# One shared PSUM pool, joined bucket bits, and DMA transposes of the attention output in a fused attention and channel-mix kernel

## The chip, the cores and the metric

The kernel runs on one core of a Trainium2 chip. The metric is device time in microseconds (us). An execution usually takes 1.7 to 2.2 us more than the span of the profile, which runs from the first to the last instruction. Runs also carry the mean clock that the throttle granted to TensorE, as a share of full speed. Some executions of a kernel take longer at a lower clock (e11: 271.86 us at 0.981, the three others 265.93 to 266.20 us at 0.991 to 0.994). Those more than 1.5% above the fastest one of the same kernel count as slow. A median that is quoted with a run is that of all its executions; ratios, and comparisons unless it is said otherwise, use the fast ones alone.

Names: PE is TensorE (matmul), PEld its weight loads, DVE is VectorE, ACT ScalarE, POOL GpSimd, SP SyncE, the engine that issues nearly all DMAs here. PSUM is the memory that the matmuls write to; this kernel divides it into eight banks, each of 512 float32 values per partition.

## The reference

Sixteen *pairs* (4 batches x 4 pairs of heads; 768 positions, head size 64) of hash-bucketed attention feed a channel mix per batch. Cut to what matters:

```python
q_bits = (np.einsum('bhsd,dk->bhsk', q, proj) > 0)      # 6 bits; the same for k
mask = q_bucket[:, :, :, None] == k_bucket[:, :, None, :]
scores = np.where(mask, scale * q @ k.T, -1e9)
attn = softmax(scores) @ v                               # per head
x = attn.transpose(0, 2, 1, 3).reshape(B, S, 512)
x_prev = x shifted by one position, zeros first
xk = mu_k * x + (1 - mu_k) * x_prev                      # xr likewise, with mu_r
k = relu(xk @ w_k); v = (k * k) @ w_v; r = sigmoid(xr @ w_r)
out = r * v
```

The first four pairs (batch 0) are computed uncentred. From pair 4 on the values are centred: the mean of v is taken off before the attention and given back later.

## The kernel before

A small planner in the kernel takes operations with durations, priorities, dependences and PSUM slots, simulates the five engines, and fixes one order per engine. Its priorities (the table `PR`) were tuned against that simulation. The operations are then issued in the planned order to a recording layer (the tile framework), which notes what each instruction reads and writes and puts in the semaphore waits.

PSUM is two tiles of two banks for scores and four tiles of one bank for everything else:

```python
sc_t = [psum.tile([P, STEP], FP32, name=f"sc{i}", tag=f"sc{i}") for i in range(2)]   # STEP = 1024
sm_t = [psum.tile([P, 512], FP32, name=f"sm{i}", tag=f"sm{i}") for i in range(4)]
plan = Plan({"sc": (2, 2), "sm": (4, 3)})

def sm(name):
    return sm_t[plan.slot[name]]
```

Bucket bits are made in two halves of 384 columns, each in one small bank. An attention output (`ob`) is turned by six PE transposes; DVE evicts it to `xt` and adds the mean in the same operation. POOL copies one column block for the shift, and DVE mixes:

```python
def ft(nm=nm):                                  # PE, six transposes
    ps = sm(nm)[:, 0:HALF].bitcast(BF16)
    for c in range(NSC):
        nc.tensor.transpose(ps[:, c * P : (c + 1) * P], ob_t[so][:, c, :], idb)
def fx(nm=nm):                                  # DVE, evicts and adds the mean
    # ... (pairs 0 to 3: a plain copy)
    nc.vector.tensor_scalar(out=xt_t[sx][:, P:], in0=sm(nm)[:, 0:HALF].bitcast(BF16),
                            scalar1=mc_t[smc][:, 0:1], scalar2=None, op0=ALU.add)
# ...
def f1(mu=mu, dst=dst):                         # DVE, mix: mu * (x - x_prev) + x; mu holds mu - 1 here
    nc.vector.scalar_tensor_tensor(out=dst[smx], in0=df_t[sd], scalar=mu[:, t : t + 1], in1=x, op0=ALU.mult, op1=ALU.add)
```

The softmax here doesn't subtract the row's maximum and nothing guards it: scores larger than these inputs give would overflow.

## Time and profile before

| | before |
|---|---|
| time, median of 3 runs | 258.73 us (258.31 to 258.94) |
| span of the profile | 256.8 us, granted clock 0.993 |
| PE busy | 239.3 us, 93% |
| first mix matmul starts | 63.4 us |

The first lines are the page's part 1 (busy time of each engine, share of the span, instructions) and part 4 (the chain of waits that ended last, as shares of the span).

```profile
PE 239.3 (93%) x2519; PEld 143.5 (56%) x2519; DVE 195.1 (76%) x391; ACT 185.5 (72%) x242; POOL 57.9 (23%) x98
...
PE 63%; DMA 15%; DVE 10%; POOL 3%; SPq 3%; issue 2%; ACT 2%; POOLq 0%; DVEq 0%
```

Next, busy time of each engine by stretches: from:to in us and its length, then us busy (instructions) of PE, PEld, DVE, ACT and POOL, the granted clock, the DMA engines' busy share and GB/s.

```profile
20.00:60.00 40.00, 34.90 (x488) 22.35 (x487) 29.58 (x54) 34.54 (x37) 10.79 (x20) 0.98 0.94 177
60.00:100.00 40.00, 38.97 (x417) 23.91 (x416) 35.89 (x75) 32.03 (x45) 13.78 (x17) 1.00 0.95 187
100.00:180.00 80.00, 78.90 (x891) 48.20 (x888) 72.84 (x142) 63.75 (x80) 20.74 (x27) 1.00 0.83 206
180.00:220.00 40.00, 40.00 (x461) 25.98 (x460) 24.77 (x59) 32.62 (x45) 1.00 (x3) 1.00 0.09 34
```

From 60 us on PE is the limit: 38.97 of 40, 78.90 of 80, 40.00 of 40 us. From 20 to 60 us only attention is ready, and ACT's exponentials (144 of 1.03 us) and PE share the work. Groups of instructions (busy us, mean ns of one | idle us of the engine just before them, and what ended it) and then waits (total us, times, longest):

```profile
L652 PE MATMUL sm<-xk,wk 128*128 128x384 bf16 x256 | 48.9, 326 | 0.2
L681 PE MATMUL sm<-wv,k 128*128 128x512 bf16 x192 | 47.8, 379 | 1.1 <-DVE ob L599 1.1
...
L583 PE MATMUL sm<-va,pt 128*128 128x65 bf16 x1152 | 44.6, 193 | 0.0
...
L674 ACT ACTIVATE rs<-sm 128x512 f32<-128x512 f32 x24 | 14.4, 599 | 22.1 <-PE sm L671 18.9
```

```profile
ACT pt L557 <- PE sc L553: 28.3, 48, 3.9
...
PE sc L553 <- ACT pt L557: 4.5, 11, 0.7
...
PE sm L681 <- DVE ob L599: 1.1, 1, 1.1
```

PE's mix matmuls (L652 and L681) idle 0.2 and 1.1 us in the whole run. PE's largest wait for another engine is for a score buffer: 4.5 us.

### The profile page before, as it was taken

Reading aid. Unit: us, or ns where it says so; the run is one execution under the profiler, and the core shown is the slowest. Engines: PE = TensorE matmul, PEld = TensorE weight load, DVE = VectorE, ACT = ScalarE, POOL = GpSimd, SP = SyncE. Lnnn points to the kernel's source line nnn. Section 1 sums busy time; section 2 is a strip of 40 time slices with the busy share of each in tenths; the row PEclk is TensorE's granted clock in tenths of the full one; section 3 lists DMA queues with packets and bytes.
Section 4 is the critical chain, followed back from the end, with each engine's and each line's share of the span. In section 5 each row is a group of like instructions: output and inputs, shape, how many; then the busy total and the mean of one; then the engine's idle time right before and its main releaser. Section 6 shows DMA issues by size and latency. Waiting matters only on the chain.

```text
span 256.8 us, 6319 instructions
## 1 busy us (share of the span) xinstructions
PE 239.3 (93%) x2519; PEld 143.5 (56%) x2519; DVE 195.1 (76%) x391; ACT 185.5 (72%) x242; POOL 57.9 (23%) x98
## 2 busy tenths in 40 slices
PE   6768898888999999999999989999999999999994
PEld 2334564555666456656666655555666666555441
DVE  4999676777789997989998999898685753675322
ACT  3838888888994598878898967586798986147320
POOL 2491415056051330504041424040000000000000
PEclk9998999999999999999999999999999999999999
DMA  6968979799998479796978987888200011220132
GB/s 191 382 168 155 163 174 172 199 171 180 225 201 227 116 199 175 212 241 190 274 148 266 216 241 149 233 164 166 89 3 6 3 41 43 82 86 1 41 123 82
DMA packets 64565, 39.78 MB, mean 155 GB/s; under 512 B 46756, under 2 KB 60952, under 8 KB 64536
## 3 DMA queue, kind: packets, MB, share of 16 engines
q1 hardware_dynamic: 62248, 36.76, 58.4%
q0 software_dynamic: 2208, 2.62, 6.3%
q8 instruction: 19, 0.31, 0.5%
q14 instruction: 10, 0.08, 0.1%
q10 hardware_dynamic: 80, 0.00, 0.0%
HBM read 24.12 MB, written 6.29 MB: 118 GB/s over the span
## 4 chain that ended last, share of the span: by engine, by line
PE 63%; DMA 15%; DVE 10%; POOL 3%; SPq 3%; issue 2%; ACT 2%; POOLq 0%; DVEq 0%
PE sc L553 16%; PE sm L681 15%; PE sm L652 11%; PE sm L583 10%; DMA vn<-in_v_dram 8%; PE sm L671 7%; PE sm L443 4%; DMA qn<-in_q_dram 3%; DMA ak<-kh 2%; POOL vt L360 2%; DMA kn<-in_k_dram 2%; PE sm L609 2%; ACT pt L557 2%; SPq L334 1%; DVE xk L635 1%
## 5 line engine op out<-in xcount | busy, mean ns | idle before, releaser
L557 ACT ACTIVATE pt<-sc 128x1024 bf16<-128x1024 f32 x144 | 143.2, 1028 | 29.9 <-PE sc L553 28.3
L553 PE MATMUL sc<-aq,ak 128*128 128x512 f16 (+1 forms) x384 | 84.6, 329 | 4.5 <-ACT pt L557 4.5
L553 PEld LDWEIGHTS <-ak 128*128 128x128 f16 x384 | 33.6, 98 | 31.1 <-issue 12.2
L652 PE MATMUL sm<-xk,wk 128*128 128x384 bf16 x256 | 48.9, 326 | 0.2
L681 PE MATMUL sm<-wv,k 128*128 128x512 bf16 x192 | 47.8, 379 | 1.1 <-DVE ob L599 1.1
L583 PEld LDWEIGHTS <-pt 128*128 128x128 bf16 x1152 | 42.9, 97 | 9.0 <-issue 0.6
L583 PE MATMUL sm<-va,pt 128*128 128x65 bf16 x1152 | 44.6, 193 | 0.0
L656 ACT ACTIVATE kr<-sm 128x384 bf16<-128x384 f32 x64 | 31.3, 498 | 9.5 <-PE sm L652 7.5
L652 PEld LDWEIGHTS <-wk 128*128 128x128 bf16 x256 | 24.1, 98 | 15.2 <-issue 0.3
L360 POOL TENSOR_TENSOR vt<-vn 128x384 f32<-128x384 f32 x12 | 15.1, 1256 | 71.5 <-DMA vn<-in_v_dram 71.5
L659 DVE TENSOR_TENSOR k<-kr 128x384 bf16<-128x384 bf16 x64 | 23.8, 385 | 8.5 <-ACT kr L656 8.4
L674 ACT ACTIVATE rs<-sm 128x512 f32<-128x512 f32 x24 | 14.4, 599 | 22.1 <-PE sm L671 18.9
L681 PEld LDWEIGHTS <-k 128*128 128x128 bf16 x192 | 18.4, 98 | 19.5 <-issue 1.3
L688 DVE SCALAR_TENSOR_TENSOR os<-rs,sm 128x512 f32<-128x512 f32 x24 | 16.3, 684 | 16.5 <-PE sm L681 16.4
L671 PE MATMUL sm<-wr,xr 128*128 128x512 bf16 x96 | 24.6, 379 | 0.0
L619 POOL COPY xt<-xt 128x127 bf16<-128x127 bf16 x16 | 8.4, 525 | 69.1 <-DVE xt L615 64.4
L447 DVE TENSOR_SCALAR bx<-sm 128x384 uint16<-128x384 uint16 (+1 forms) x32 | 16.4, 549 | 3.3 <-PE sm L443 2.6
L599 DVE TENSOR_TENSOR ob<-sm,rc 128x384 bf16<-128x384 f32 x32 | 17.8, 556 | 0.9
L405 DVE SCALAR_TENSOR_TENSOR kh<-kn,kh 128x768 f16<-128x768 f32 x15 | 18.3, 1219 | 0.1
L635 DVE SCALAR_TENSOR_TENSOR xk<-df,muk,xt 128x768 bf16<-128x768 bf16 x16 | 16.7, 1046 | 0.3
L443 PE MATMUL sm<-ak,p 128*32 128x384 f16 x124 | 14.4, 335 | 2.3 <-DVE ak L422 1.3
L635 DVE SCALAR_TENSOR_TENSOR xr<-df,mur,xt 128x768 bf16<-128x768 bf16 x16 | 16.1, 1018 | 0.0
(76 smaller groups left out, 195.3 us busy)
## 6 DMA issues: line engine op xcount, KB each, us to landing
vn<-in_v_dram SPq DMA_DIRECT2D x16, 384.0 KB
out_dram<-os SPq DMA_DIRECT2D x24, 256.0 KB
qn<-in_q_dram SPq DMA_DIRECT2D x15, 384.0 KB
kn<-in_k_dram SPq DMA_DIRECT2D x15, 384.0 KB
wk<-in_moe_w_k_dram POOLq DMA_DIRECT2D x4, 256.0 KB, 5.3
wv<-in_moe_w_v_dram POOLq DMA_DIRECT2D x4, 256.0 KB, 8.7
wr<-in_moe_w_r_dram POOLq DMA_DIRECT2D x2, 256.0 KB, 5.4
aq<-bx SPq DMA_DIRECT2D x31, 9.0 KB
```

Of the source, the lines that this page charges most:

```text
L360: nc.gpsimd.tensor_tensor(out=vt[:, :, :, 0:E], in0=src[:, :, 0:3, 0:E], in1=src[:, :, 3:6, 0:E], op=ALU.add)
L405: nc.vector.scalar_tensor_tensor(out=nh[:, :, D:P], in0=nat.rearrange("p j (c d) -> p (j c) d", d=D), scalar=QS, in1=nh[:, :, 0:D], op0=AL ...
L443: nc.tensor.matmul(ps[32 * i : 32 * i + 32, 0:HALF], w_, a[:, i // 2, h * HALF : (h + 1) * HALF], start=st, stop=not st)
L553: nc.tensor.matmul(ps[:, lo - s * STEP : hi - s * STEP], side_a["k"][sa][:, j, jc * P : (jc + 1) * P], side_a["q"][sa][:, j, q0 : q0 + hi ...
L557: nc.scalar.activation(out=pt_t[sp][:, s * STEP : (s + 1) * STEP], in_=sc_t[plan.slot[nm]], func=AF.Exp, bias=EBIAS, scale=ESC)
L583: nc.tensor.matmul(oo[:, ic * 65 : ic * 65 + 65], pt_t[sp][:, o : o + P], va_t[sa][:, j, jc, 0 : D + 1], start=(not uc and ic == 0 and jc ...
L635: nc.vector.scalar_tensor_tensor(out=dst[smx], in0=df_t[sd], scalar=mu[:, t : t + 1], in1=x, op0=ALU.mult, op1=ALU.add)
L652: nc.tensor.matmul(ps[:, 0:HALF], wk_sb[:, d, fc * P : (fc + 1) * P], xk_t[mx[d]][:, h * HALF : (h + 1) * HALF], start=(d == 0), stop=(d = ...
L656: nc.scalar.activation(out=kr_t[sk], in_=sm(nm)[:, 0:HALF], func=AF.Relu, scale=0.5 ** 0.5)
L659: nc.vector.tensor_tensor(out=k2_t[s2][:, h * HALF : (h + 1) * HALF], in0=kr_t[sk], in1=kr_t[sk], op=ALU.mult)
L671: nc.tensor.matmul(sm(nr), xr_t[mx[d]][:, c * P : (c + 1) * P], wr_sb[:, d, :], start=(d == 0), stop=(d == NDC - 1))
L681: nc.tensor.matmul(sm(nv), k2_t[(b * NFC + fc) % NK2][:, c * P : (c + 1) * P], wv_sb[:, fc, :], start=(fc == 0), stop=(fc == NFC - 1))
```

## The change

Its intent: (1) one PSUM pool of four two-bank tiles. Scores take whole tiles, up to three at a time, and small outputs take halves of tiles. (2) The bucket bits of a pair are made in one two-bank tile and read by one DVE operation. (3) The outputs of pairs 4 to 14 are turned by DMA transposes, not by PE. (4) x stays centred, since the DVE eviction that added the mean falls away; the mean is added in the mix, by a `tensor_scalar` with two scalars and a `tensor_tensor`, and POOL writes minus the mean in front of the first position. (5) All priorities are tuned again. The diff, cut to its core (planner bookkeeping and names left out):

```diff
-    sc_t = [psum.tile([P, STEP], FP32, ...) for i in range(2)]
-    sm_t = [psum.tile([P, 512], FP32, ...) for i in range(4)]
-    plan = Plan({"sc": (2, 2), "sm": (4, 3)})
+    ps_t = [psum.tile([P, STEP], FP32, name=f"ps{i}", tag=f"ps{i}") for i in range(4)]
+    plan = Plan((0, 1, 2), (7, 6, 5, 4), {"sc": 3, "sm": 4}, 3)
     def sm(name):
-        return sm_t[plan.slot[name]]
+        b_ = plan.slot[name]
+        return ps_t[b_ // 2][:, (b_ % 2) * 512 : (b_ % 2) * 512 + 512]
...
-        for h in range(2):
-            nm = f"bits{n}_{h}"          # 384 columns each, in a small bank
+        nm = f"bits{n}"                  # 768 columns, in a two-bank tile
...
+    OT_PE = (0, 1, 2, 3, 15)
+        def fd_():
+            nc.sync.dma_start_transpose(out=xt_t[sx][:, P:].rearrange("p (c q) -> p c q", q=P),
+                                        in_=ob_t[so].rearrange("p c d -> p (c d)"))
+        if n in OT_PE:
             # six PE transposes and a DVE copy, as before
+        else:
+            add("SP", 1.2, n + PR["otd"], fd_, r=[("ob", so, 0), ("ob", so, 1)], w=[("xt", sx)], ...)
...
-                nc.vector.scalar_tensor_tensor(out=dst[smx], in0=df_t[sd], scalar=mu[:, t : t + 1], in1=x, ...)
+                nc.vector.tensor_scalar(out=tm_t[tm], in0=df_t[sd], scalar1=mu[:, t : t + 1], scalar2=mc[:, 0:1], op0=ALU.mult, op1=ALU.add)
+                nc.vector.tensor_tensor(out=dst[smx], in0=tm_t[tm], in1=x, op=ALU.add)
```

## The prediction

> **What bounds the kernel now.** TensorE, from about 60 us on: the windows show PE busy 19.2 to 20.0 of every 20 us (18.9 once). Busy times of pipelined matmuls overlap, so I check with start-to-start times from the timeline (384 columns 0.162 us, 512 columns 0.216, a 65-column attention matmul 0.0316, a 1024-column score step 0.43, 16 bucket-bit matmuls 0.77, six transposes 0.335). With the counts per window these sum to about 152 us of the last 157: PE is 97% full. Over the whole span (256.8 us) they sum to about 225. The other 32 us are the start (some 12), the attention-only stretch of 20 to 60 us (some 9: no mix matmul is ready, ACT does exponentials of 1.03 us, busy 34.5 of 40), small gaps and the tail. In that stretch ACT loses 5.5 us, nearly all waiting for scores (waits): there are two score buffers, and 36 attention matmuls take 1.14 us, longer than one exponential.
>
> **What the change does.**
> - PE: 11 of 16 output transposes leave (pairs 4 to 14): 11 x 0.335 = 3.7 us, in the full stretch, so nearly all counts.
> - DVE: 11 evictions of 0.61 us leave (6.7). Bucket bits: two of 0.55 become one of about 0.95 (-2.4 in all). [...] In sum -12 of 195 us, mostly off the critical path: PE hardly waits for DVE.
> - DMA: 11 transposes of 192 KB. Those of before (384 KB) move about 210 GB/s with the queue full (174 to 176 us), where stores reach 400 (184 us): about 0.9 us each, 10 us between 75 and 185 us, where the share is about 0.85; it rises to about 0.95. [...] SP gains about 1 us of issue per pair.
> - PSUM: scores may hold three buffers, though the joined bits borrow one about 2 us per pair. From 20 to 60 us this should return 1 to 2.5 us of ACT's idle time, and start the first mix earlier by that.
>
> **Sum.** 3.7 us of PE work and 1.5 us of early idle time, less 0.3 us for late DMAs: 258.7 - 4.9 = 253.8 us. Range 250.0 to 257.5. Faster by over 2% (below 253.6) 0.46, within 2% 0.48, slower 0.06.
>
> **What would show it.** 30 output transposes on PE instead of 96; PE still full after 60 us; ACT's wait for scores from 20 to 60 us below 5.5; first mix matmul before 63 us; [...] DVE busy near 183; DMA share near 0.95 from 80 to 180 us; new waits of POOL's copy or df for a DMA, but few of PE.
>
> **What would make it wrong.** Queued transposes delaying the query and key transposes behind them, so that PE, in its fixed order, stalls on scores; SP waiting in order for an attention output and holding back loads; joined bits taking a score buffer when it is needed; shared banks adding waits between mix and scores; or the retuned priorities being worth more than I give them, seen as less idle time before 60 us.

The forecast's DVE sum came to -12 us, and its "DVE busy near 183" is 195 less that; only 9.1 us of it stand above (6.7 for evictions, 2.4 for bits), since the mix's term is cut. The 253.8 us is whole: no term of 3.7, 1.5 and 0.3 us is cut. The 0.95 us for the joined bits was an estimate; before's trace gives about as much (384 columns 549 ns, one column of another `tensor_scalar` out of PSUM, the mean's, 146: twice the difference and 146 make 952).

## The result, and the profile after

| | before | after |
|---|---|---|
| time, median | 258.60 us (258.31 to 258.94, 4 runs) | 289.77 us (289.29 to 291.15, 4 runs, all fast) |
| span, granted clock | 256.8 us, 0.993 | 287.5 us, 0.982 |
| PE busy | 239.3 us, 93% | 246.0 us, 86% |
| first mix matmul | 63.4 us | 72.2 us |

The ratio is 1.12 (95% interval 1.116 to 1.124). Ratios here and below are the mean time of one kernel's fast runs over that of the other's fast runs in the same rounds, so they are not quite the ratio of the medians quoted.

The same views of the kernel after, in the same order:

```profile
PE 246.0 (86%) x2453; PEld 142.9 (50%) x2453; DVE 189.8 (66%) x388; ACT 183.9 (64%) x242; POOL 60.8 (21%) x110
...
PE 53%; DVE 23%; DMA 10%; ACT 5%; issue 5%; POOL 1%; SPq 1%; ACTq 0%; DVEq 0%; POOLq 0%
```

```profile
20.00:60.00 40.00, 31.72 (x426) 20.74 (x426) 27.52 (x45) 28.54 (x31) 12.65 (x21) 0.91 0.88 180
60.00:100.00 40.00, 35.00 (x369) 21.20 (x368) 28.00 (x59) 31.93 (x44) 14.85 (x22) 0.96 0.79 166
100.00:180.00 80.00, 70.38 (x768) 41.80 (x767) 60.95 (x129) 55.92 (x71) 16.32 (x27) 1.00 0.73 176
180.00:220.00 40.00, 36.77 (x375) 21.68 (x374) 30.07 (x68) 27.77 (x38) 5.53 (x10) 1.00 0.59 138
```

```profile
L690 PE MATMUL ps<-xk,wk 128*128 128x384 bf16 x256 | 49.1, 329 | 4.9 <-ACT kr L694 2.2
L719 PE MATMUL ps<-wv,k 128*128 128x512 bf16 x192 | 47.6, 378 | 5.2 <-ACT rs L712 2.4
...
L601 PE MATMUL ps<-va,pt 128*128 128x65 bf16 x1152 | 48.4, 195 | 8.7 <-DVE va L404 2.3
...
L712 ACT ACTIVATE rs<-ps 128x512 f32<-128x512 f32 x24 | 14.4, 600 | 35.5 <-DVE os L726 15.1
```

```profile
ACT rs L712 <- DVE os L726: 15.1, 5, 3.3
...
PE ps L596 <- DVE ob L617: 5.2, 3, 2.2
...
PE ps L719 <- ACT rs L712: 2.4, 5, 0.7
...
PE ps L601 <- DVE va L404: 2.3, 4, 0.7
...
PE ps L719 <- DVE ob L617: 2.0, 4, 1.1
```

The loss is spread over the whole kernel: from 60 to 220 us PE was busy 142.15 us, not 157.87 (sums of the three stretches). PE's share of the chain fell from 63% to 53%, and DVE's rose from 10% to 23%. DMA did not take it: its busy share from 100 to 180 us fell from 0.83 to 0.73.

The waits name the reason. L719 is the last matmul of the channel mix, `k2 @ w_v`. It reads `k2` and `wv`; it does not read `rs` (ACT's gate, L712) or `ob` (an attention output, L617). Yet it waits for both. L712 is an evicting activation with two output buffers, and it waits 15.1 us for L726, DVE's product of another PSUM output. These are not waits for a free buffer: in the built program, each of the 7 has L712 writing one buffer while L726 reads the other. None of the five kinds of wait shown is in the list of before, except L681's single 1.1 us on `ob`. The timeline of one stretch shows it at work (start, us, instruction, and in brackets the engine's idle time before it and what ended it):

```profile
115.28 0.17 DVE L612 TENSOR_SCALAR rc<-ps 128x6 f32<-128x6 f32 x1 [1.33 <-PE ps L719]
115.48 0.19 DVE L613 RECIPROCAL rc<-rc 128x6 f32<-128x6 f32 x1
115.71 0.56 DVE L617 TENSOR_TENSOR ob<-ps,rc 128x384 bf16<-128x384 f32 x1
...
116.32 1.02 PE L719 MATMUL ps<-wv,k 128*128 128x512 bf16 x4 [1.07 <-DVE ob L617]
```

DVE normalises an attention output (L612, L613, L617; 115.28 to 116.27 us) out of one half of a two-bank tile. PE's next matmuls go into a different bank, the other half, and start 0.05 us after DVE is done. They had waited 1.07 us. DVE itself had idled 1.33 us before L612, released by PE's matmuls L719, whose result it doesn't read.

### The profile page after: what moved, and what is told of

Same layout as the page of the kernel before. It is cut to its first block, busy times and chain, and to the rows that moved or that the text cites. A ratio compares the mean times of both kernels' runs of the same rounds, so it can differ in the third digit from the quotient of the medians.

```text
span 287.5 us, 6215 instructions
## 1 busy us (share of the span) xinstructions
PE 246.0 (86%) x2453; PEld 142.9 (50%) x2453; DVE 189.8 (66%) x388; ACT 183.9 (64%) x242; POOL 60.8 (21%) x110
## 2 busy tenths in 40 slices
DMA packets 73366, 41.94 MB, mean 146 GB/s; under 512 B 55557, under 2 KB 69753, under 8 KB 73337
## 4 chain that ended last, share of the span: by engine, by line
PE 53%; DVE 23%; DMA 10%; ACT 5%; issue 5%; POOL 1%; SPq 1%; ACTq 0%; DVEq 0%; POOLq 0%
PE ps L719 12%; PE ps L571 10%; PE ps L690 10%; PE ps L601 9%; PE ps L709 6%; DMA qn<-in_q_dram 5%; PE ps L462 4%; DVE kh L424 3%; DVE ob L617 3%; ACT kr L694 3%; DVE va L404 3%; DMA vn<-in_v_dram 3%; DVE os L726 2%; DVE qh L424 2%; DVE qh L421 2%
## 5 line engine op out<-in xcount | busy, mean ns | idle before, releaser
L575 ACT ACTIVATE pt<-ps 128x1024 bf16<-128x1024 f32 x144 | 140.2, 1029 | 33.6 <-PE ps L571 32.9
L571 PE MATMUL ps<-aq,ak 128*128 128x512 f16 (+1 forms) x384 | 80.0, 330 | 2.3 <-DVE bx L465 1.5
L601 PEld LDWEIGHTS <-pt 128*128 128x128 bf16 x1152 | 45.8, 99 | 27.7 <-issue 19.6
L601 PE MATMUL ps<-va,pt 128*128 128x65 bf16 x1152 | 48.4, 195 | 8.7 <-DVE va L404 2.3
L690 PE MATMUL ps<-xk,wk 128*128 128x384 bf16 x256 | 49.1, 329 | 4.9 <-ACT kr L694 2.2
L719 PE MATMUL ps<-wv,k 128*128 128x512 bf16 x192 | 47.6, 378 | 5.2 <-ACT rs L712 2.4
L694 ACT ACTIVATE kr<-ps 128x384 bf16<-128x384 f32 x64 | 29.3, 492 | 24.0 <-PE ps L690 14.7
L712 ACT ACTIVATE rs<-ps 128x512 f32<-128x512 f32 x24 | 14.4, 600 | 35.5 <-DVE os L726 15.1
L719 PEld LDWEIGHTS <-k 128*128 128x128 bf16 x192 | 18.2, 97 | 26.3 <-issue 8.0
L726 DVE SCALAR_TENSOR_TENSOR os<-rs,ps 128x512 f32<-128x512 f32 x24 | 16.4, 682 | 21.6 <-PE ps L709 12.6
L709 PE MATMUL ps<-wr,xr 128*128 128x512 bf16 x96 | 24.6, 378 | 0.8 <-DVE ob L617 0.6
L617 DVE TENSOR_TENSOR ob<-ps,rc 128x384 bf16<-128x384 f32 x32 | 17.8, 556 | 4.8 <-PE ps L690 1.7
L465 DVE TENSOR_SCALAR bx<-ps 128x768 uint16<-128x768 uint16 (+1 forms) x16 | 15.3, 955 | 6.6 <-PE ps L462 6.3
L404 DVE SCALAR_TENSOR_TENSOR va<-ps,vn 128x384 bf16<-128x384 f32 x24 | 12.9, 553 | 8.9 <-ACT pt L575 2.2
L462 PE MATMUL ps<-aq,p 128*32 128x512 f16 (+1 forms) x124 | 15.1, 353 | 0.7 <-DVE bx L465 0.3
```

The costliest lines, as they stand in the source:

```text
L462: nc.tensor.matmul(ps[32 * i : 32 * i + 32, lo:hi], w_, a[:, i // 2, lo:hi], start=st, stop=not st)
L571: nc.tensor.matmul(ps[:, lo - s * STEP : hi - s * STEP], side_a["k"][sa][:, j, jc * P : (jc + 1) * P], side_a["q"][sa][:, j, q0 : q0 + hi ...
L575: nc.scalar.activation(out=pt_t[sp][:, s * STEP : (s + 1) * STEP], in_=ps_t[plan.slot[nm]], func=AF.Exp, bias=EBIAS, scale=ESC)
L601: nc.tensor.matmul(oo[:, ic * 65 : ic * 65 + 65], pt_t[sp][:, o : o + P], va_t[sa][:, j, jc, 0 : D + 1], start=(not uc and ic == 0 and jc ...
L617: nc.vector.tensor_tensor(out=ob_t[so][:, :, j * D : (j + 1) * D], in0=oo[:, :, 0:D], in1=rc_t[sr][:, 1, :].unsqueeze(2).to_broadcast([P, ...
L690: nc.tensor.matmul(ps[:, 0:HALF], wk_sb[:, d, fc * P : (fc + 1) * P], xk_t[mx[d]][:, h * HALF : (h + 1) * HALF], start=(d == 0), stop=(d = ...
```

## The experiments

**Theory 1: shared tiles.** Two halves of one tile are different banks to the planner, but the recording layer makes accesses of one half wait for accesses of the other. The planner knows banks singly, so its order neither expects nor avoids these waits. **Rivals.** Theory 2: the DMA transposes come late or hold up loads. Theory 3: the retuned order or the joined bits starve PE by themselves.

A count comes first, since it costs no run. In the built programs I resolved each semaphore wait to the instruction that it waits for, and noted where their only common memory is the *other* half of a PSUM tile:

```
kernel                                         waits resolved   other half only
before                                         1142             0
before with its small banks as halves (e2)     1096             205
after                                          1089             140
after, waits between halves declared away (e1) 1150             8
```

The 8 left belong to whole-tile operations. When this text was checked, the kernels were built again and counted with a slightly wider rule, which also takes two reads of one tile: 0, 235, 162 and 11. By it all 7 waits of L712 on L726 are of this kind, though both only read the tile, and so are all 6 of L601 on L404, 4 of 8 of L719 on L712, 2 of 4 of L719 on L617, 2 of 4 of L596 on L617 and 1 of 3 of L612 on L719. The others wait for the same half, as they must. So most, not all, of the waits shown above are of this kind. Whether they cost 31 us only a run can tell.

### e1: after, without the waits between halves

The same instructions in the same order on every engine; the layer is told that an access of one half need not wait for accesses of the other half, but for those that the plan itself orders (cut to its core, comments added):

```diff
         for o in order:
             o.fn()
+            # got: the instructions just issued; b_: the bank of this small output
+            # keep: instructions of the operations that the plan orders before this one
+            for e in ("PE", "ACT", "DVE"):
+                if e != o.eng and (b_ ^ 1, e) in members:
+                    for x in got:
+                        tc.declare_no_dep(x, group=f"bank{b_ ^ 1}{e}", keep=held, ...)
+            for x in got:
+                tc.add_to_no_dep_group(f"bank{b_}{o.eng}", x)
```

> The kernel after, same instructions in the same order on every engine, but the waits between the two single-bank halves of a shared PSUM tile are taken out (only those: waits for the same bank and for SBUF data stay; resolved in the built program, waits whose only link is the other half of a PSUM tile fall from 140 to 8). Theory 1 (shared tile makes the two halves wait for each other): 251 to 260 us, PE gaps after 100 us nearly gone. Rival 2 (DMA transposes in the ordered SP queue delay query/key/x): 282 to 290 us. Rival 3 (new order, priorities and joined bits): 282 to 290 us.

Measured: 262.75 us median (260.23 to 265.05), 261.94 over the three fast runs, ratio to before 1.0099 (1.0024 to 1.0174). The result was correct. The profiled run was the slow one (265.05 us, clock 0.974), so its windows probably understate the gain:

```profile
60.00:100.00 40.00, 38.02 (x458) 24.74 (x457) 31.90 (x68) 35.62 (x50) 15.73 (x24) 1.00 0.93 190
100.00:180.00 80.00, 76.13 (x813) 45.12 (x811) 64.66 (x140) 60.92 (x77) 15.29 (x28) 0.98 0.79 180
```

PE's 35.00 us became 38.02, and 70.38 became 76.13. Taking these waits away, and nothing else, removes about 11 of the 12 per cent. Theory 1 holds for the bulk, and theories 2 and 3 fall for it, as e1 keeps the DMA transposes, the retuned order and the joined bits, and they expected 282 to 290 us. What is left, about 1% above before where 2% below was predicted and above the 251 to 260 us expected here, needs another reason.

### e2: before, with its small banks as halves

```diff
-    sm_t = [psum.tile([P, 512], FP32, name=f"sm{i}", tag=f"sm{i}") for i in range(4)]
+    sm_p = [psum.tile([P, STEP], FP32, name=f"sm{i}", tag=f"sm{i}") for i in range(2)]
+    sm_t = [sm_p[i // 2][:, 512 * (i % 2) : 512 * (i % 2) + 512] for i in range(4)]
```

> The kernel before, same instructions in the same order, but its four one-bank PSUM tiles are declared as halves of two two-bank tiles, as the change declares them (waits linked only by the other half: 205 instead of 0). Theory 1: 275 to 300 us. Rivals 2 and 3: 258 to 260 us, as nothing they name is touched.

Measured: 285.95 us (285.61 to 287.09), ratio 1.1033 (1.0983 to 1.1084). This kernel has before's order, bits, PE transposes and mix; only how four banks are declared differs, and it loses 10%. The same kinds of wait appear (L657 is `kr`, L600 is `ob`, L675 is `rs`, L689 is `os`; in the recount 7 of the 12 waits of L675 on L689 are for the other half alone):

```profile
ACT rs L675 <- DVE os L689: 6.1, 3, 3.5
ACT kr L657 <- DVE ob L600: 5.9, 7, 1.8
```

So the cost does not need any other part of the change.

### e3 and e4: all output transposes on PE

```diff
-    OT_PE = (0, 1, 2, 3, 15)
+    OT_PE = tuple(range(16))
```

e3 does this to the kernel after, e4 to e1's.

> The kernel after with all 16 output transposes on PE again (no DMA transpose of outputs), shared PSUM tiles kept. Theory 1: 283 to 296 us. Rival 2: 256 to 266 us. Rival 3: 283 to 296 us.

> The same as e3, all output transposes on PE, with the cross-half waits taken out as in e1. The difference from e1 is what the DMA transposes are worth without the false waits. My prediction's sum puts them at 3 to 4 us of PE work: e1 plus 3 to 5 us, 255 to 263 us under theory 1. If DMA transposes cost time by themselves, this is faster than e1. Rival 3: still above 280 us.

Measured: e3 292.37 us (290.81 to 293.23), ratio 1.1253 (1.1189 to 1.1317); e4 267.61 us (263.62 to 269.14), ratio 1.0232 (1.0131 to 1.0333). Theory 2 falls as the reason for the slowdown: with no DMA transpose of outputs at all, e3 is as slow. The 265.37 us of e4's two fast runs (263.62 and 267.11) lie above the 255 to 263 expected, as e1 itself came out higher. Under the retuned order the transposes on DMA gain about 3.4 us: 265.37 less 261.94, medians of the fast runs, and as much between the runs of both at full clock (263.62 and 260.23). That is near the 3.7 us predicted, but it rests on two and three runs whose ranges touch (263.62 and 263.56).

### e5 and e6: before's order, and split bits (wrong results)

e5 is e1 with before's priorities; e6 is e1 with the bits in two halves again, each in a small bank.

> e1 (no cross-half waits) with the 34 priorities of the kernel before in place of the retuned ones; shared banks, joined bits and DMA transposes stay. It tells why e1 starts its first mix matmul at 68.6 us where before does at 63.4. If the retuned order is to blame: first mix matmul back to 60 to 64 us, no stretch at half clock beyond 24 us. If joined bits or the third score buffer are to blame: 66 to 70 us again. The total may be long (259 to 270 us), as these priorities were not tuned for this structure.

> e1 with the bucket bits in two halves in one-bank buffers, as before; retuned priorities and DMA transposes stay. If joined bits cause the late first mix: 61 to 65 us. If the retuned order does: 66 us or later. Total 258 to 270 us.

Both gave *wrong results* (relative errors 0.032 and 0.040), with times of 270.12 and 269.51 us. New orders had laid open a gap that the plan of both kernels has. The small DVE operation that stores the mean gives a PSUM bank back, but is not ordered behind the two that centre the values from the same bank. The orders of before and after happen to be safe (e2 and e1 keep them, and are correct). e9 and e10 repeat these two with the gap closed, and their numbers replace these.

### e9, e10 and e11: the same, mended, and the early order without DMA transposes

```diff
-        add("DVE", DVE_C(1), n + PR["va"], f6, r=[(nm,)], w=[("mc", sm_)], give=[nm])
+        add("DVE", DVE_C(1), n + PR["va"], f6, r=[(nm,), ("va", sa, 0), ("va", sa, 1)], w=[("mc", sm_)], give=[nm])
```

e11 is e9 with all outputs turned on PE (e3's edit).

> The kernel of e5 (the changed kernel without the waits between halves, with the priorities of before) gave a wrong result. In the plan, the small operation that stores the mean gives the PSUM bank back but is not ordered behind the two that centre the values; in that order another write may reach the bank before they read it. Here that one order is added to the plan. If this is the fault, the result is right (in the simulator it is). The retuned order is to blame for the late first mix matmul: still 62 to 65 us. If losing the retuned order costs more later than it gives early: 264 to 272 us, as e5.

> The kernel of e6 (bucket bits in two halves of one bank each) with the same order added. The result is right if that was the fault. If the joined bits were what delays the first mix matmul: 62 to 66 us; if not, as in e6: 69 us or later. Time 258 to 262 if split bits help, 264 to 271 if they don't.

> As e9, but with all 16 output transposes on PE: what is left of the change is the shared pool (third score buffer), the joined bits and the centred x. If the DMA transposes are what stretches 60 to 180 us under the early order (PE busy 71.9 of 80 us from 100 to 180 in e5): PE busy of 100 to 180 goes up to 75 or more and the time falls below e9 by 3 us or more. If they save PE time there too: slower than e9 by 3 to 6 us.

| | time (us), median of all 4 | ratio, 95% | first mix matmul | PE busy 100 to 180 |
|---|---|---|---|---|
| e9 | 271.56 | 1.0449 (1.0368 to 1.0531) | 63.3 | 72.31 |
| e10 | 264.91 | 1.0196 (1.0106 to 1.0287) | 75.3 | 76.62 |
| e11 | 266.17 | 1.025 (1.0135 to 1.0364) | 63.9 | 76.56 |

All three are correct with this one order added, which fits the gap as the fault. (e10 and e11 each hold one slow run; their fast medians are 264.40 and 266.14.) Two things follow. First, the late first mix matmul comes from the retuned order: 68.6 us in e1, though in a slow run, against 63.3 in e9 with before's order; between two fast profiles with all transposes on PE, 66.6 in e4 against 63.9 in e11. Split bits do not bring it back (75.3). Second, the DMA transposes have no value of their own, apart from an order. Under the retuned order they gain 3.4 us (e4 to e1); under before's order they cost 5.4 (e11 to e9, medians of the fast runs). Why e11, without waits between halves and without DMA transposes, is still 6 us slower than before is not settled; three parts differ at once and its order was not tuned for them.

### e7: the DMA transposes and centred x alone, on before's tiles

Separate tiles, split bits and two score buffers as in before; DMA transposes, centred x and the two-step mix as in after; the priorities searched anew in the planner, which left before's early order in place.

> The DMA transposes and the centred mix alone, on the kernel before: its separate PSUM tiles, its split bits, its order of the first 50 us (the other priorities searched anew in the kernel's own planner). If the DMA transposes are worth what my sum said (3.7 us of PE) and the early stretch is unchanged: 254 to 257 us, first mix matmul at 62 to 65 us. If DMA transposes cost time by queueing: 259 us or more.

Measured: 259.31 us (258.8 to 261.2), ratio 1.0009 (0.9951 to 1.0067): not the gain, but the expectation's other branch. PE busy did fall, from 239.3 to 236.1 us, close to the 3.7 predicted (the trace lacks 18 of the 2453 matmul records, so the fall is at most this). But the span did not (257.6 us). From 100 to 120 us PE is busy 17.14 us where before has 20.00. The chain of waits there (start, us, what):

```profile
105.18 0.57 DVE ob L601
...
105.77 1.42 SPq L617
...
107.28 4.32 DMA vn<-in_v_dram
...
111.74 1.08 POOL vt L362
...
114.21 0.22 PE sm L381
```

The attention output is done at 105.75; SP issues its transpose for 1.42 us, and behind it the value load at 107.28; POOL sums the values when they land, and PE's mean matmul waits for that until 114.21. In before the value loads of this stretch were issued at 100.04 and 111.20 us, with no output transpose near them.

### e8: e1 with its priorities searched anew

The search used the planner with added DMA latency, to get an order that suffers less from late loads. The edit is the table `PR` alone.

> An attempt to beat both kernels: e1 with priorities searched again in the planner, with 0, 0.5 and 1 us more of DMA latency than it assumes, so that the order suffers less from late loads. If late loads in a fixed order cause e1's residue: 252 to 259 us. If not, 260 us or more.

Measured: 259.14 us (259.01 to 259.28), ratio 0.9991 (0.9943 to 1.0039). First mix matmul at 67.1 us; PE busy 78.43 from 100 to 180. So all parts of the change together, without the waits between halves and in a better order, come out level with before. This points to the order, not the parts, as the remaining 1% of e1; the two intervals overlap slightly (e1 from 1.0024, e8 up to 1.0039).

### e12: e7 with loads ahead of transposes

Only SP's order changes, in 7 places where a load stood directly behind an output transpose:

```diff
     order = plan.schedule()
+    for o in [o for o in order if o.name.startswith("otd")]:
+        i = order.index(o)
+        for k in range(i + 1, len(order)):
+            x = order[k]
+            if x.eng != "SP":
+                continue
+            if x.svc == 1.15 and all(order.index(plan.ops[d]) < i for d in x.deps):
+                order.insert(i, order.pop(k))      # x is a load: ahead of the transpose
+            break
```

> The kernel of e7 (separate tiles, DMA transposes, centred x) with one thing changed, in the sync engine's order alone: where a load stood directly behind an output transpose (7 places), it goes ahead of it. In e7 the chain of waits from 104.96 to 114.21 us runs from an attention output, through the issue of its transpose, to a value load issued behind it at 107.28 us, and to TensorE, which was busy 17.14 of the 20 us from 100 to 120 (20.00 in before). If that queueing is what took back the 3.2 us that TensorE saved: busy over 19 of 20 us there, and 255.5 to 257.5 us, 1 to 1.5 percent below before. If the loads only come late somewhere else, or the transposes themselves are late instead: the time stays at 258.5 to 260.

Measured (5 rounds): 259.45 us (258.2 to 260.46), ratio 0.9996 (0.9944 to 1.0048): a miss again. The load in question did go out earlier, at 104.68 us, but PE was still busy only 16.56 of 20 us. POOL's timeline shows why:

```profile
109.83 0.38 POOL L624 COPY xt<-xt 128x127 bf16<-128x127 bf16 x1 [8.88 <-DMA xt<-ob]
110.17 1.00 POOL L362 TENSOR_TENSOR vt<-vn 128x384 f32<-128x384 f32 x1
```

SP issued the transpose at 106.52 us and it landed at 109.8, 3.3 us later. POOL works in its fixed order, and the shifting copy of the transposed output (L624) stands ahead of the value sums. It idled 8.88 us, so the sums started at 110.17 although the load had been issued 2.6 us earlier than in e7. Of these 8.88 us only the last 3.3 are the transpose. The first 5.6 passed before it was issued, while DVE had not finished the attention output (106.50 us), and a transpose on PE would have had to wait for that as well. So the second reading named in the expectation holds: what stands behind a late transpose on another engine waits. How much of PE's loss is the 3.3 us of DMA and how much is POOL's order, no run separates. No version here beats before by a margin outside its interval.

## Why the prediction was wrong, point by point

- **Failed step: the PSUM item.** The prediction says that "scores may hold three buffers" and that this "should return 1 to 2.5 us of ACT's idle time". It costs the pool's capacity, and leaves its waits to a clause among the risks: "shared banks adding waits between mix and scores". The risk was near but not at the spot: no bank is shared. Halves of one tile are treated as one, and mix, attention outputs, transposes and value centring wait for each other. Measured: 140 such waits in the program; 1.12 falls to 1.01 when they go (e1: about 28 of the 31 us), and before rises to 1.10 when it gets them (e2). So the item put down as a gain of 1 to 2.5 us was nearly the whole loss. The diff shows `sm()` returning a slice of a two-bank tile; the right question was what the layer tracks: tiles or banks.
- **No gain from the third score buffer shows.** ACT was busy 34.54 us from 20 to 60 us before and 28.54 after. Its waits for scores there, listed for that stretch, were 8.0 us before, 11.3 after, and 8.3 even in e11, which has three buffers, before's priorities and no false waits. No run has the third buffer alone; the joined bits, which borrow one, are in e11 too. (The prediction's 5.5 us is 40 less ACT's busy time; a wait in the list may reach out of the stretch.) "Below 5.5" and "first mix matmul before 63 us" (72.2) were both wrong.
- **"PE still full after 60 us" was wrong**: 142.15 of 160 us to 220 us, as above.
- **PE's saving was right in size, wrong as a saving of time.** 30 output transposes on PE, as said, and PE busy up to 3.2 us lower in e7. The step "in the full stretch, so nearly all counts" failed: it takes the other engines' timing as fixed. e7 and e12 give it all back as PE idle time, e1 keeps about 3.4 us against e4, e9 loses 5.4 us against e11.
- **DMA was dearer than estimated, but not the limit.** Predicted 10 us for 11 transposes and a share near 0.95. Busy time of the main queue, as share times span, rises by 18.0 us from before to e7 (65.2% of 257.6 less 58.4% of 256.8), by 15.7 from e4 to e1 (61.5% of 263.3 less 55.1% of 265.3) and by 10.5 from e11 to e9 (59.3% of 270.0 less 56.6% of 264.4). Eleven transposes of 192 KB in 10.5 to 18.0 us are 120 to 206 GB/s by estimate (2.16 MB over these times); stores in before's trace reached 410 GB/s (184.0 to 184.5 us). From before to after, the packets under 512 bytes rose by 8,801 (46,756 to 55,557). SP's issue of one output transpose took 1.22 to 1.88 us (nine of them in the kernel after), where about 1 was predicted. The share from 100 to 180 us was 0.73 in the kernel after. In e7 and e8, as fast as before, it was 0.84, where before has 0.83: what was added shows from 180 to 220 us, with 0.49 and 0.42 against 0.09.
- **DVE was right in direction.** The joined bits take 955 ns as said (about 0.95), the mix's second step 0.55 to 0.64. The `tensor_scalar` takes 0.472 and 0.487 us (means of its two groups in the kernel after); the duration predicted for it rested on no trace. DVE busy was 189.8 us, and 187.3 in e1, where 183 was predicted, with the cut term in it.
- **The retuned priorities were only considered as a possible gain.** ("being worth more than I give them, seen as less idle time before 60 us") In the early stretch they cost: the first mix matmul is 2.7 us later in e4 (66.6) than in e11 (63.9), both fast, and 5.3 us later in e1 (68.6, slow) than in e9 (63.3). The planner that they were tuned in does not know the waits between halves. One suspect is that in e1 SP issues two long transposes before the bits' rows. (Start, us, instruction, from SP's timeline of e1:)

```profile
18.68 3.32 SPq L428 DMA_TRANSPOSE aq<-qh  x1
22.11 2.45 SPq L428 DMA_TRANSPOSE ak<-kh  x1
24.65 0.72 SPq L478 DMA_DIRECT2D aq<-bx  x1
```

In before the rows of this stretch go out from 21.30, with one transpose ahead. But e8, level with before, has the same pair of transposes at the same place in SP's order (in its built program), so they alone do not make a kernel slow. PE also has gaps. The longest of this stretch in e1 ended with the output transposes of an early pair (L628), which stand at this place in PE's order and waited for DVE's attention output (L618). First comes that line of PE's timeline, then the windows around it, with the granted clock as the third number from the end:

```profile
45.49 0.51 PE L628 MATMUL ps<-idb,ob 128*128 128x128 bf16 x6 [2.27 <-DVE ob L618]
...
42.00:44.00 2.00, 1.22 (x8) 0.56 (x6) 1.97 (x3) 1.83 (x3) 1.25 (x2) 1.00 1.27 275
44.00:46.00 2.00, 0.51 (x7) 0.45 (x8) 1.40 (x3) 1.31 (x2) 0.00 (x0) 0.97 0.53 106
46.00:48.00 2.00, 2.00 (x10) 0.94 (x9) 1.54 (x3) 1.09 (x2) 1.34 (x3) 0.50 1.53 191
```

PE was busy 0.51 of 2 us, and the clock of the next 2 us was 0.50, after a gap of 2.27 us, which is all that PE lacked in the 4 us before (2 less 1.22, and 2 less 0.51). A gap does not always bring it: in the kernel after, one of 2.44 us ends at 139.20, and the clock stays at 1.00 from 136 to 146 us. This profile of e1 is of a slow run; the fast profile of the kernel after shows the same gap (2.49 us, to 45.02) and a clock of 0.58 from 46 to 48, and the fast profile of e9, with before's order, has a mean clock of 0.96 from 20 to 60 us and of 0.98 from 100 to 180. So a lowered clock does not tell the two orders apart, as the expectation of e5 had it (before's own was 0.56 and 0.58 in the windows from 18 to 22 us, and 1.00 from 22 to 72). That the order delays the first mix is shown (e11 against e4, e9 against e1); which part of it does is not settled.

## What to carry to other kernels

When small outputs move into slices of larger tiles, find out at what grain the framework tracks them before counting on the freed space: declare one tile per unit that should be independent, or declare the independence, and count the waits in the built program. Work taken off the full engine became no time in e7 (PE busy up to 3.2 us lower, ratio 1.0009), as other things in the fixed orders moved with it. The operation put on DMA brought its latency (3.3 us from issue to landing, once, in e12), and POOL, whose order has the value sums behind that result, waited for it; look for such engines before counting on the gain. Judge such a part under an order tuned for it: the same 11 transposes moved the time by -3.4 us (e4 to e1), about 0 (before to e7) and +5.4 us (e11 to e9).
